# A hop-token graph transformer: a third buffer for the big one-hot of the second bucket pass, shared buffers for its smaller tiles, and slot rows asked for in the other order

## The chip, the cores and the metric

The kernel runs on one core of one Trainium2 chip. The metric is the device time of one execution in microseconds (us); the time given is the median of several runs. A profile comes from one execution more, taken by the hardware profiler.

## What is computed

The reference, cut to what matters (N = 10000 nodes, E = 160000 edges with random ends, D = 128, K = 7):

```python
h = x
toks = [x]
for _ in range(K):
    msg = h[src] * deg_inv_sqrt[src, None] * deg_inv_sqrt[dst, None]
    h = _segment_sum(msg, dst, N)
    toks.append(h)
tok = jnp.stack(toks, axis=1)                      # (N, K+1, D)
t = _layernorm(tok, axis=-1)
# q, key, v = t @ wq, t @ wk, t @ wv
attn = _softmax(jnp.einsum('nkd,nld->nkl', q, key) * scale, axis=-1)
o = tok + jnp.einsum('nkl,nld->nkd', attn, v) @ wo
alpha = _softmax(jnp.einsum('nkd,d->nk', _layernorm(o, axis=-1), w_r), axis=-1)
return jnp.einsum('nk,nkd->nd', alpha, o)
```

Seven times the rows of the nodes are gathered by src, weighted, and summed by dst; then each node's eight tokens go through one attention block and a weighted sum.

## The kernel before

The edges never move as rows. They are sorted once into buckets, and each hop is then done by matmuls with one-hot matrices. Four stretches follow one another:

- **First bucket pass** (`pass_a`): edges are bucketed by the 128-node tile of dst; there are 79 such tiles (NT). `decode` turns the result into keys.
- **Second bucket pass and first hop**, interleaved (`run`, the loop over quads). This is where the change lies.
- **Hops 2 to 7**: for each tile a matrix w is loaded, rows of the table are gathered with it by matmuls (L608), copied from PSUM (eb, L613 and L615) and summed into the tile (acc, L583).
- **Attention**, with an order of its own written out by hand.

In the second pass the edges of each dst tile are bucketed again by blocks of the source node (76 buckets, NS, of 32 slots, CAP). Tiles are taken in *quads* of four, and a quad is placed as two *pairs*. `place` does a quad. For each pair, with DVE unless another engine is named: the big one-hot `oh` (128 x 25 x 76 x 2, in two buffers) by `onehot` (L213) from the keys; PE counts it (ur, L430, L436), ACT copies the counts (H, U2); in `rank` the product `ux` of oh and U2 (L226), PE sums it (L230, L231), DVE reduces it to the ranks rk (L234); the one-hot `rob` of the ranks (L213), and its two products with the slot values, both halves of `R` (L219). Then PE places: `tb` = oh x R in 50 small matmuls (L449), and ACT copies tb (tbs, L450). At the end of the quad the slot rows go to DRAM (`srow`, L459), and a handful of overflow edges per tile is treated with small steps and two one-hots `ohp` (L493).

`matrices` builds for each of the 79 tiles the matrix w that the hops use: it reads the tile's slot row back, spread over all partitions, in two pieces `ra` (two buffers) and `rb` (one buffer), both asked for on SP's queue (L517). rb becomes a part of w on DVE (L524), ra two parts on ACT (L529), dsl another on DVE (L532), and w is written to DRAM (gsd, L534). `hop1` runs the first hop over the finished tiles of an earlier quad (`block`, `fin1`).

Three generators, placing quad q+1, building the matrices of quad q and the first hop of quad q-1, are stepped in turn, 16 rounds a quad:

```python
for i in range(16):
    if i % 3 != 1:
        next(pl, None)
    if i % 4 < 3:
        next(mt, None)
    next(hp, None)
```

One tile of `matrices` is three steps: L524 with the request of the next tile's row and half of L529; the other half; L532 with the write of w. One tile of the hop is four steps.

This order is only a preference. When the kernel is built, a list scheduler lays the instructions of each engine in a fixed order by estimated durations, buffers that come free and, among those ready, place in the program. Each engine then works off its list in order and waits on semaphores.

Pools: `bwp` holds two buffers of each of its tiles, `bw1` one. A tile is known by its name, or by its tag where one is given; tiles of one tag share the buffers.

Of the kernel before, what the change touches and what calls it, by code (L numbers as in the profile page):

```python
# [8 lines left out]
F16 = mybir.dt.float16  # L9
# [19 lines left out]
NCH = NCOL // B  # L29
CAP = 32  # L30
NJ = NG + NI
NS = 4 * NJ
# [4 lines left out]
KO = 8  # L37
# [10 lines left out]
class Hops:  # L48
# [158 lines left out]
            V.tensor_copy(self.q2, q[:, 0:1])  # L207


    def onehot(self, pool, name, key, n):  # L210
        m = key.shape[1]
        oh = pool.tile([128, m, n, 2], F16, name=name)
        self.nc.vector.tensor_tensor(oh, key[:, :, None, :].to_broadcast([128, m, n, 2]),  # L213
                                     self.io2[:, None, :n, :].to_broadcast([128, m, n, 2]), op=ALU.is_equal)
        return oh
# [4 lines left out]

    def rank(self, wp, wu, R, oh, U2, w):

        nc, T = self.nc, self.nc.tensor
        m, nk, k = oh.shape[1], oh.shape[2], 5
        ux = wu.tile([128, m, nk, 2], F16, name="ux")
        nc.vector.tensor_tensor(ux, oh, U2[:, None].to_broadcast([128, m, nk, 2]), op=ALU.mult)  # L226
        R = R[:, :m * k * 2].rearrange("p (j k i) -> p j k i", k=k, i=2)
        for s in range(0, nk, k):
            e = min(k, nk - s)
            T.matmul(R[:, :, :e, :], self.id16, ux[:, :, s:s + e, :], start=s == 0, stop=False, skip_group_check=True)  # L230
        T.matmul(R[:, :, 0, :], self.id16, w, start=False, stop=True, skip_group_check=True)  # L231
        rk = wp.tile([128, m, 2], F16, name="rk")
        with nc.allow_low_precision("whole numbers; those over 2048 only have to stay large"):
            nc.vector.tensor_reduce(rk, R.rearrange("p j k i -> p j i k"), axis=X, op=ALU.add)  # L234
        return rk
# [182 lines left out]
    def place(self, ts, got):  # L418

        tc, nc, V, A, T, G = self.tc, self.nc, self.nc.vector, self.nc.scalar, self.nc.tensor, self.nc.gpsimd  # L420
        wp, w1, n = self.bwp, self.bw1, len(ts)
        tbs = wp.tile([NS, 4, 64], F16, name="tbs")
        ov = wp.tile([128, 4, 8], F32, name="ov")
        for p0 in range(0, n, 2):
            cols = lambda z: z[:, :, ts[0] + p0:ts[0] + p0 + 2]
            oh = self.onehot(wp, "oh", cols(self.kB), NS)
            ur = self.pU.tile([128, 512], F32, name="ur")
            H = wp.tile([128, NS, 2], F16, name="H")
            for c in range(NCH):
                T.matmul(ur[:, :2 * NS], self.id16, oh[:, c], start=c == 0, stop=c == NCH - 1)  # L430
            A.copy(H, ur[:, :2 * NS].rearrange("p (k i) -> p k i", i=2))
            yield
            U = ur[:, 512 - 2 * NS:].rearrange("p (k i) -> p k i", i=2)
            h = NS // 4
            for w in range(4):
                T.matmul(U[:, w * h:(w + 1) * h], self.triw[:, w, :], H[:, w * h:(w + 1) * h], start=True, stop=True)  # L436
            U2 = wp.tile([128, NS, 2], F16, name="U2")
            A.copy(U2, U)
            yield
            rk = self.rank(wp, w1, ur, oh, U2, cols(self.wB))  # L440
            ro = self.onehot(w1, "rob", rk, CAP)
            R = w1.tile([128, NCH, 2 * CAP, 2], F16, name="R")
            self.times(R[:, :, :CAP], ro, cols(self.sl))
            self.times(R[:, :, CAP:], ro, cols(self.dl))
            yield
            tb = self.psm.tile([NS, 2, 64], F32, name="tb")
            for g in range(2):
                for c in range(NCH):
                    T.matmul(tb[:, g, :], oh[:, c, :, g], R[:, c, :, g], start=c == 0, stop=c == NCH - 1)  # L449
            A.copy(tbs[:, p0:p0 + 2, :], tb)  # L450
            vo = wp.tile([128, NCH, 2], F32, name="vo")
            V.scalar_tensor_tensor(vo, rk, float(CAP), cols(self.TT), op0=ALU.is_ge, op1=ALU.mult)
            for g in range(2):
                V.max(ov[:, p0 + g, :], vo[:, :, g])
            yield
        n, a, b = len(ts), ts[0], ts[-1] + 1
        msc = self.psm.tile([128, 128], F32, name="msc")

        nc.sync.dma_start(self.srow[a:b, :].rearrange("t (s r) -> s t r", r=CAP), tbs[:4 * NG, :n, 0:CAP])  # L459
        dsl = wp.tile([128, 4, NJ], F16, name="dsl")  # L460
        for g in range(n):
            for q in range(4):
                T.matmul(msc[32 * q:32 * q + 32, 32 + g * NJ:32 + (g + 1) * NJ], tbs[:, g, CAP:2 * CAP], self.esel[:, q, :],
                         start=True, stop=True, tile_position=(0, 32 * q))
                T.matmul(msc[32 * q:32 * q + 32, 16 + g * NI:16 + (g + 1) * NI], tbs[:, g, 0:CAP], self.esel[:, q, NG:],
                         start=True, stop=True, tile_position=(0, 32 * q))
        A.copy(dsl[:, :n, :], msc[:, 32:32 + n * NJ].rearrange("p (g j) -> p g j", j=NJ))
        V.tensor_scalar(self.oidx[:, a:b, :NI], msc[:, 16:16 + n * NI].rearrange("p (g i) -> p g i", i=NI), -1.0, 0.0, op0=ALU.add, op1=ALU.max)
        got.append(dsl)
        n = 4  # L470

        fl = wp.tile([128, 4, 8], F16, name="fl")
        V.tensor_scalar(fl[:, :n], ov[:, :n], 0.5, None, op0=ALU.is_gt)
        ct = wp.tile([128, 4], F16, name="ct")
        with self.nc.allow_low_precision("counts up to 8"):
            V.tensor_reduce(ct[:, :n], fl[:, :n], axis=X, op=ALU.add)
        T.matmul(msc[:, 0:n], self.tri, ct[:, :n], start=True, stop=True)
        yield
        po = wp.tile([128, 4, 8], F32, name="po")
        V.tensor_tensor(po[:, :n], msc[:, 0:n, None].to_broadcast([128, n, 8]), self.iof1[:, None, :8].to_broadcast([128, n, 8]), op=ALU.add)  # L480
        V.tensor_mul(po[:, :n], po[:, :n], fl[:, :n])
        ph = wp.tile([128, KO, 4], F16, name="ph")
        V.tensor_scalar(ph.rearrange("p k g -> p g k"), po[:, :n, :KO], -1.0, None, op0=ALU.add)
        vi = wp.tile([128, 4, 8, 4], I32, name="vi4")
        V.tensor_scalar(vi[:, :n, :, 3], ov[:, :n], -1.0, None, op0=ALU.add)
        V.tensor_single_scalar(vi[:, :n, :, 0], vi[:, :n, :, 3], 14, op=ALU.arith_shift_right)
        V.tensor_scalar(vi[:, :n, :, 1], vi[:, :n, :, 3], 7, 127, op0=ALU.arith_shift_right, op1=ALU.bitwise_and)  # L487
        V.tensor_single_scalar(vi[:, :n, :, 2], vi[:, :n, :, 3], 127, op=ALU.bitwise_and)
        dg = wp.tile([128, 4, 8, 3], F16, name="dg")
        V.tensor_copy(dg[:, :n, :, 0:2], vi[:, :n, :, 0:2])  # L490
        V.tensor_scalar(dg[:, :n, :, 2], vi[:, :n, :, 2], 1.0, None, op0=ALU.add)
        for g in range(0, n, 2):
            ohp = self.onehot(w1, "ohp", ph[:, :, g:g + 2], 128)  # L493
            for i in range(2):
                for k in range(KO):
                    T.matmul(msc[:, 4 + 3 * (g + i):7 + 3 * (g + i)], ohp[:, k, :, i], dg[:, g + i, k, :], start=k == 0, stop=k == KO - 1)
        yield
        lo = wp.tile([128, 16], F32, name="lo")
        V.tensor_copy(lo[:, :3 * n], msc[:, 4:4 + 3 * n])
        l3 = lo[:, :12].rearrange("p (g k) -> p g k", k=3)  # L500
        n = len(ts)
        V.scalar_tensor_tensor(self.oidx[:, a:b, NI], l3[:, :n, 0], 128.0, l3[:, :n, 1], op0=ALU.mult, op1=ALU.add)
        V.tensor_tensor(self.Sov[:, a:b, :], l3[:, :n, 2:3].to_broadcast([128, n, 128]),
                        self.iof1[:, None, :].to_broadcast([128, n, 128]), op=ALU.is_equal, saturate=False)

    def matrices(self, ts, dsl, W):
# [4 lines left out]
        def row(t):  # L511
            m = 4 * NA * CAP
            ra = self.bwp.tile([128, m], F16, name="ra")
            rb = self.bw1.tile([128, 4 * NG * CAP - m], F16, name="rb")
            r1 = self.srow[t:t + 1, :]
            for r, a in ((ra, 0), (rb, m)):
                nc.sync.dma_start(r, bass.AP(tensor=r1.tensor, offset=r1.offset + a, ap=[[0, 128], [1, r.shape[1]]]))  # L517
            return ra, rb

# [137 lines left out]
    def run(self, ctx, att, nhop=K):  # L657
        tc, nc, V, A, T, G = self.tc, self.nc, self.nc.vector, self.nc.scalar, self.nc.tensor, self.nc.gpsimd
        with ExitStack() as c:
# [46 lines left out]
            for q in range(nq + 1):  # L706
# [5 lines left out]
                for i in range(16):  # L712
                    if i % 3 != 1:
                        next(pl, None)
                    if i % 4 < 3:
                        next(mt, None)
                    next(hp, None)
                for g in (pl, mt, hp):
# [655 lines left out]
```

## Time and profile before

| | |
|---|---|
| median of 3 runs | 3949.62 us (3941.75 to 3951.11) |
| the profiled execution | 3958.33 us, its span 3956.4 us |
| PE busy over the span | 3707.2 us (94%) |
| DVE busy | 3165.6 us (80%) |
| ACT busy | 2812.9 us (71%) |
| POOL busy | 1689.8 us (43%) |
| second pass with first hop, 404 to 1150 us | PE 676.05, DVE 663.59, ACT 551.17, POOL 251.31 us busy |

PE is TensorE, DVE VectorE, ACT ScalarE, POOL GpSimd, SP the engine that issues most DMAs. Busy time is the union of an engine's instructions. A wait is told as "who <- whom": the instruction that stood at the head of its engine, and the one whose end released it, with the idle time in us, the number of times and the longest. A row of the timeline has start and duration in us, engine, line, operation, written <- read tiles, shapes and count; in brackets the idle time ahead of it and what ended it.

### The profile page before, as it was taken

Reading aid. Unit: us, or ns where it says so; the run is one execution under the profiler, and the core shown is the slowest. Engines: PE = TensorE matmul, PEld = TensorE weight load, DVE = VectorE, ACT = ScalarE, POOL = GpSimd, SP = SyncE. Lnnn points to the kernel's source line nnn. Section 1 sums busy time; section 2 is a strip of 40 time slices with the busy share of each in tenths; the row PEclk is TensorE's granted clock in tenths of the full one; section 3 lists DMA queues with packets and bytes.
Section 4 is the critical chain, followed back from the end, with each engine's and each line's share of the span. In section 5 each row is a group of like instructions: output and inputs, shape, how many; then the busy total and the mean of one; then the engine's idle time right before and its main releaser. Section 6 shows DMA issues by size and latency. Waiting matters only on the chain.

```text
span 3956.4 us, 174256 instructions
## 1 busy us (share of the span) xinstructions
PE 3707.2 (94%) x74141; PEld 2992.0 (76%) x74141; DVE 3165.6 (80%) x6888; ACT 2812.9 (71%) x6950; POOL 1689.8 (43%) x2221
## 2 busy tenths in 40 slices
PE   6787899999989999999999999999999998999997
PEld 4665677777768888888888788878878886777775
DVE  8998999998867777777777777777776664888888
ACT  6885577777776666766667677666765657888885
POOL 0000234333345665666566566656656662121111
PEclk8998899999999999999999999999999999999998
DMA  3100454545456666666666666666666653222220
GB/s 101 37 2 1 146 160 152 164 148 158 142 160 191 199 202 194 203 200 203 192 198 203 183 205 203 198 191 198 203 191 202 189 183 98 83 76 84 77 83 18
DMA packets 332729, 595.58 MB, mean 151 GB/s; under 512 B 57447, under 2 KB 215493, under 8 KB 326693
## 3 DMA queue, kind: packets, MB, share of 16 engines
q1 hardware_dynamic: 293989, 506.70, 40.6%
q0 software_dynamic: 35392, 72.55, 6.7%
q8 instruction: 580, 9.50, 1.0%
q10 hardware_dynamic: 2560, 5.12, 0.5%
q14 instruction: 208, 1.70, 0.2%
HBM read 455.49 MB, written 128.67 MB: 148 GB/s over the span
## 4 chain that ended last, share of the span: by engine, by line
PE 72%; DVE 16%; DMA 5%; ACT 3%; issue 2%; SPq 1%; another core or an unknown queue 0%; ACTq 0%; DVEq 0%; POOLq 0%
PE p L608 26%; PE acc L583 23%; PE acc L568 4%; PE pv L1018 4%; PE pu L1002 3%; DMA rb<-srow 2%; DVE o L219 2%; DVE w L532 2%; DVE oh L213 2%; DVE ux L226 2%; PE po L1037 2%; PE tb L449 2%; PE pt L992 2%; PE ps L1067 1%; ACT rs L347 1%
## 5 line engine op out<-in xcount | busy, mean ns | idle before, releaser
L613 ACT ACTIVATE eb<-p 128x512 f16<-128x512 f32 x3065 | 1636.7, 604 | 566.2 <-PE p L608 327.9
L615 DVE TENSOR_TENSOR eb<-p,four 128x512 f16<-128x512 f32 x1912 | 1232.0, 686 | 334.8 <-PE acc L583 201.3
L608 PE MATMUL p<-tab,w 128*32 128x256 f16 x39816 | 1296.2, 275 | 42.8 <-issue 15.3
L608 PEld LDWEIGHTS <-w 128*32 128x32 fp8e4 x39816 | 998.9, 96 | 231.6 <-issue 171.4
L583 PE MATMUL acc<-eb,w 128*128 128x256 f16 x8532 | 1013.6, 273 | 0.7 <-issue 0.7
L583 PEld LDWEIGHTS <-w 128*128 128x128 fp8e4 x8532 | 836.7, 98 | 99.9 <-issue 1.3
L544 POOL DMA_INDIRECT og<-tabh,oidx x553 | 626.1, 1132 | 662.3 <-DVE vi L487 388.3
L544 POOL DMA_INDIRECT og<-tabd,oidx x541 | 553.4, 1023 | 752.2 <-PE acc L566 311.8
L653 POOL TENSOR_SCALAR r<-s,ctok 128x128 f32<-128x128 f32 x474 | 294.9, 622 | 48.7 <-DVE s L599 31.1
L644 ACT ACTIVATE tab<-s,c 128x128 f16<-128x128 f32 x395 | 158.5, 401 | 204.0 <-DVE eb L615 167.7
L645 DVE SCALAR_TENSOR_TENSOR tab<-s,c,tab 128x128 f16<-128x128 f32 x395 | 138.9, 352 | 180.6 <-issue 168.8
L1107 POOL TENSOR_TENSOR p<-e,in 128x1024 f32<-128x1024 f32 (+1 forms) x40 | 76.5, 1913 | 447.0 <-DVE e L1106 447.0
L1059 ACT ACTIVATE junk<-tab 128x128 f32<-128x128 f32 x626 | 248.6, 402 | 8.4 <-SPq L1343 6.8
L347 ACT ACTIVATE rs<-iof,rb 128x128 fp8e4<-128x128 f32 x784 | 231.8, 389 | 0.3
L599 DVE TENSOR_REDUCE s<-acc 128x128 f32<-128x256 f32 x474 | 196.8, 415 | 24.8 <-PE acc L597 11.7
L558 PE MATMUL acc<-eb,w 128*128 128x129 f16 x1422 | 214.5, 225 | 1.8 <-ACT eb L613 1.7
L532 DVE TENSOR_TENSOR w<-dsl,iof 128x2432 fp8e4<-128x2432 f16 x79 | 211.9, 2683 | 0.8 <-PE acc L559 0.8
L559 PE MATMUL acc<-eb,w 128*128 128x128 f16 x1422 | 210.7, 222 | 0.0
L558 PEld LDWEIGHTS <-w 128*128 128x128 fp8e4 x1501 | 140.1, 98 | 65.8 <-issue 62.9
L543 POOL COPY og<-eb 128x1 f16<-128x1 f16 x452 | 84.1, 186 | 240.2 <-ACT eb L613 240.1
L1018 PEld LDWEIGHTS pv<-Wv,xT 128*64 128x64 f32 x2504 | 138.9, 137 | 44.7 <-ACT uT L1003 29.1
L1018 PE MATMUL pv<-Wv,xT 128*64 128x131 f32 x2504 | 163.6, 280 | 8.4 <-issue 4.6
(299 smaller groups left out, 5048.7 us busy)
## 6 DMA issues: line engine op xcount, KB each, us to landing
w<-gsd SPq DMA_DIRECT2D x474, 592.0 KB
gsd<-w SPq DMA_DIRECT2D x79, 592.0 KB
tok<-r SPq DMA_DIRECT2D x546, 64.0 KB
tab<-tok SPq DMA_DIRECT2D x273, 128.0 KB
tabd<-tab SPq DMA_DIRECT2D x396, 64.0 KB
ra<-srow SPq DMA_DIRECT2D x79, 320.0 KB
rb<-srow SPq DMA_DIRECT2D x79, 256.0 KB
og<-tabh,oidx POOLq DMA_INDIRECT x553
```

What stands on the lines that cost most here:

```text
L347: A.activation(ro[:, j - a, i, :], self.iof, AF.Abs_reciprocal_sqrt, scale=2.0 ** 21, bias=rb[:, j - VP, i:i + 1], saturate=False)
L532: V.tensor_tensor(w[:, :NJ * 128].rearrange("p (j d) -> p j d", d=128), dsl[:, g, :, None].to_broadcast([128, NJ, 128]), self.iof1[:, None ...
L544: self.nc.gpsimd.indirect_dma_start(out=o, out_offset=None, in_=src[0] if i == NI else src[1], in_offset=bass.IndirectOffsetOnAxis(ap=self ...
L558: T.matmul(acc[0][:, :128 + ones], W, rows[:, 128:256 + ones], start=start, stop=False, skip_group_check=True)
L559: T.matmul(acc[0][:, :128], W, rows[:, :128], start=False, stop=False, skip_group_check=True)
L583: T.matmul(acc[0][:, :256], w[:, J * 128:(J + 1) * 128], e[:, j, :256], start=False, stop=J == NG - 1 and not late)
L608: T.matmul(p[32 * q:32 * q + 32, j], w[:, NJ * 128 + s * CAP:NJ * 128 + (s + 1) * CAP], tab[:, s, :], start=True, stop=True)
L613: A.activation(e[:, :n, 0:256], pv, AF.Copy, scale=4.0)
L615: V.tensor_tensor(e[:, :n, 0:256], pv, self.four[:, :, None].to_broadcast([128, n, 256]), op=ALU.mult)
L653: self.nc.gpsimd.tensor_scalar(r, s, ct[:, t:t + 1], None, op0=ALU.mult)
L1018: T.matmul(p[64 * h:64 * h + 64, u - us[0], :], S[i]["xT"][:, h * m + q, 64 * c:64 * c + 64], Wv, start=True, stop=True, tile_position=(0, ...
L1059: A.activation(j, S[i]["x"][:, g, :], AF.Square, bias=S[i]["x"][:, g, 0:1], scale=-1.0, accum_out=R[i % 6][:, 0, g:g + 1])
```

## The change

- `oh` of the second pass gets three buffers instead of two.
- `rob` and `ohp` share one buffer (tag "ohp"), of ohp's size; `R` and `ux` share one buffer (tag "ux"), of ux's size. R is the first 64 of 76 columns of such a tile, so its rows stand 304 bytes apart instead of 256. In bytes per partition: oh 7600 more, rob's 3200 and R's 6400 of their own are no longer needed.
- For each row rb is asked for ahead of ra.
- The steps of `matrices` stand in rounds 1, 2, 3 of each four, instead of 0, 1, 2.

The tiles of `onehot` are allocated flat and viewed in the old shape. The number of instructions and their shapes stay.

```diff
@@ -207,9 +207,9 @@
             V.tensor_copy(self.q2, q[:, 0:1])
 
 
-    def onehot(self, pool, name, key, n):
+    def onehot(self, pool, name, key, n, size=None, **kw):
         m = key.shape[1]
-        oh = pool.tile([128, m, n, 2], F16, name=name)
+        oh = pool.tile([128, size or 2 * m * n], F16, name=name, **kw)[:, :2 * m * n].rearrange("p (m n i) -> p m n i", n=n, i=2)
         self.nc.vector.tensor_tensor(oh, key[:, :, None, :].to_broadcast([128, m, n, 2]),
                                      self.io2[:, None, :n, :].to_broadcast([128, m, n, 2]), op=ALU.is_equal)
         return oh
@@ -222,7 +222,7 @@
 
         nc, T = self.nc, self.nc.tensor
         m, nk, k = oh.shape[1], oh.shape[2], 5
-        ux = wu.tile([128, m, nk, 2], F16, name="ux")
+        ux = wu.tile([128, m, nk, 2], F16, name="ux", tag="ux")
         nc.vector.tensor_tensor(ux, oh, U2[:, None].to_broadcast([128, m, nk, 2]), op=ALU.mult)
         R = R[:, :m * k * 2].rearrange("p (j k i) -> p j k i", k=k, i=2)
         for s in range(0, nk, k):
@@ -423,7 +423,7 @@
         ov = wp.tile([128, 4, 8], F32, name="ov")
         for p0 in range(0, n, 2):
             cols = lambda z: z[:, :, ts[0] + p0:ts[0] + p0 + 2]
-            oh = self.onehot(wp, "oh", cols(self.kB), NS)
+            oh = self.onehot(wp, "oh", cols(self.kB), NS, bufs=3)
             ur = self.pU.tile([128, 512], F32, name="ur")
             H = wp.tile([128, NS, 2], F16, name="H")
             for c in range(NCH):
@@ -438,8 +438,8 @@
             A.copy(U2, U)
             yield
             rk = self.rank(wp, w1, ur, oh, U2, cols(self.wB))
-            ro = self.onehot(w1, "rob", rk, CAP)
-            R = w1.tile([128, NCH, 2 * CAP, 2], F16, name="R")
+            ro = self.onehot(w1, "rob", rk, CAP, 2 * KO * 128, tag="ohp")
+            R = w1.tile([128, NCH, NS, 2], F16, name="R", tag="ux")[:, :, :2 * CAP]
             self.times(R[:, :, :CAP], ro, cols(self.sl))
             self.times(R[:, :, CAP:], ro, cols(self.dl))
             yield
@@ -490,7 +490,7 @@
         V.tensor_copy(dg[:, :n, :, 0:2], vi[:, :n, :, 0:2])
         V.tensor_scalar(dg[:, :n, :, 2], vi[:, :n, :, 2], 1.0, None, op0=ALU.add)
         for g in range(0, n, 2):
-            ohp = self.onehot(w1, "ohp", ph[:, :, g:g + 2], 128)
+            ohp = self.onehot(w1, "ohp", ph[:, :, g:g + 2], 128, tag="ohp")
             for i in range(2):
                 for k in range(KO):
                     T.matmul(msc[:, 4 + 3 * (g + i):7 + 3 * (g + i)], ohp[:, k, :, i], dg[:, g + i, k, :], start=k == 0, stop=k == KO - 1)
@@ -513,7 +513,7 @@
             ra = self.bwp.tile([128, m], F16, name="ra")
             rb = self.bw1.tile([128, 4 * NG * CAP - m], F16, name="rb")
             r1 = self.srow[t:t + 1, :]
-            for r, a in ((ra, 0), (rb, m)):
+            for r, a in ((rb, m), (ra, 0)):
                 nc.sync.dma_start(r, bass.AP(tensor=r1.tensor, offset=r1.offset + a, ap=[[0, 128], [1, r.shape[1]]]))
             return ra, rb
 
@@ -712,7 +712,7 @@
                 for i in range(16):
                     if i % 3 != 1:
                         next(pl, None)
-                    if i % 4 < 3:
+                    if i % 4:
                         next(mt, None)
                     next(hp, None)
                 for g in (pl, mt, hp):
```

## The prediction

> **What bounds the kernel now.** I read the page first, then the engines' busy time by stretches (the columns are the stretch, its length, the busy time of PE, weight loads, DVE, ACT and POOL, the granted clock and the DMA share), then the waits, the chain and the timeline of the stretch that the edit touches.
>
> ```profile
> span 3956.4 us, 174256 instructions
> ```
> ```profile
> 404.00:1150.00 746.00, 676.05 (x13392) 530.55 (x13393) 663.59 (x977) 551.17 (x1148) 251.31 (x152) 0.97 0.50 157
> ```
>
> The edit touches the second bucket pass, which shares its stretch (404 to 1150 us) with the first hop. That is 746 us of 3956; later hops keep their instructions, and in the first pass only the way a tile is named differs. PE is busy for 676 us and DVE for 664 of these 746, so neither is full: DVE lacks 82 us, PE 70. What fills the gaps is read from the waits of the same stretch (us in total, times, longest):
>
> ```profile
> DVE w L524 <- DMA rb<-srow: 30.5, 26, 2.8
> DVE oh L213 <- PE tb L449: 25.6, 20, 3.3
> PE tb L449 <- DVE R L219: 23.1, 23, 2.3
> PE p L608 <- ACT eb L613: 13.4, 26, 2.0
> PE msc L496 <- DVE ohp L213: 12.4, 26, 1.9
> PE p L608 <- ACT w L529: 5.9, 2, 5.1
> PE ur L230 <- DVE ux L226: 2.7, 4, 1.5
> ACT w L529 <- DMA ra<-srow: 26.8, 18, 6.0
> SPq L655 <- ACT r L651: 204.8, 62, 8.8
> ```
>
> Two waits hold 56 of DVE's 82 idle us: the slot row rb (30.5) and the big one-hot oh, which waits for the place matmuls tb (25.6). PE in its turn waits 38 us for DVE (23.1 + 12.4 + 2.7). Whether DVE sets the pace is a matter of the chain of waits; these are pieces of it (start, us, what):
>
> ```profile
> 805.69 2.08 PE tb L449 x50
> 807.79 2.14 DVE oh L213
> ...
> 823.16 0.67 DVE w L524
> 823.85 4.24 DMA rb<-srow
> 828.11 0.75 DVE w L524
> ...
> 831.75 2.00 PE tb L449 x50
> ```
>
> Between 807.8 and 823.8 the chain is almost all DVE, and it leaves DVE just at the two waits: through tb into oh, and through the transfer of rb from one L524 to the next. So these waits are on the path, not beside it. The timeline shows how they arise:
>
> ```profile
> 807.79 2.14 DVE L213 TENSOR_TENSOR oh<-kB,io 128x3800 f16<-128x3800 f16 x1 [0.88 <-PE tb L449]
> ...
> 823.08 0.75 DVE L524 TENSOR_SCALAR w<-rb,pid 128x1024 fp8e4<-128x1024 f16 x1
> ...
> 828.11 0.75 DVE L524 TENSOR_SCALAR w<-rb,pid 128x1024 fp8e4<-128x1024 f16 x1 [1.29 <-DMA rb<-srow]
> 828.78 0.98 DVE L213 TENSOR_TENSOR rob<-rk,io 128x1600 f16<-128x1600 f16 x1
> 829.68 0.20 DVE L452 SCALAR_TENSOR_TENSOR vo<-rk,TT 128x50 f32<-128x50 f16 x1
> 829.81 0.99 DVE L219 TENSOR_TENSOR R<-rob,sl 128x1600 f16<-128x1600 f16 x1
> 830.71 0.98 DVE L219 TENSOR_TENSOR R<-rob,dl 128x1600 f16<-128x1600 f16 x1
> ...
> 831.80 2.12 DVE L226 TENSOR_TENSOR ux<-oh,U 128x3800 f16<-128x3800 f16 x1
> 833.83 2.13 DVE L213 TENSOR_TENSOR oh<-kB,io 128x3800 f16<-128x3800 f16 x1
> ...
> 870.21 2.14 DVE L213 TENSOR_TENSOR oh<-kB,io 128x3800 f16<-128x3800 f16 x1 [1.90 <-PE tb L449]
> ...
> 872.34 2.13 DVE L226 TENSOR_TENSOR ux<-oh,U 128x3800 f16<-128x3800 f16 x1
> ```
>
> After the products R of a pair DVE has one of two orders. Either ux of the next pair follows at once, beside tb (831.80), and oh comes behind it without a wait (833.83); or oh comes first and waits for tb, because with two buffers its own is the one that tb still reads (870.21, 1.90 us), and ux follows (872.34). With the second pair of a quad some small steps lie between R and oh, and 0.88 us of the wait is left (807.79).
>
> **The third buffer.** It adds no instruction. oh of 2.14 us depends on nothing but kB and a free buffer, so with a third one it can be laid into the 2.0 us in which tb runs. The ends: all 25.6 us of DVE idle time go, or none, if the order fills the third buffer earlier and the next oh then waits for tb as before. No other engine is asked for more: PE reads the same tiles.
>
> **The shared buffers.** rob shares with ohp, R with ux. rob is read by DVE alone (the two products behind it, 829.81 and 830.71), and ohp is read by 16 short matmuls far from any rob, so I put nothing on that pair. The cover is that distance; without it a rob would wait for matmuls that now themselves wait for ohp, 12.4 us in 26 places, and that is the end of what it could cost. R and ux are another matter. R is written behind its own ux anyway. But ux of the next pair may now start only when tb has read R, and in the first order above it runs just beside tb. I count nine such places, these being the first and the last of them:
>
> ```profile
> 455.22 2.13 DVE L226 TENSOR_TENSOR ux<-oh,U 128x3800 f16<-128x3800 f16 x1
> ...
> 1066.64 2.12 DVE L226 TENSOR_TENSOR ux<-oh,U 128x3800 f16<-128x3800 f16 x1
> ```
>
> Nine times the 2.00 us of tb is 18 us of new wait, with ux at the head of DVE and rob, L524 and L532 queued behind it, if nothing stands ahead of it. If oh of 2.14 us is laid there, the order is R, oh, ux, and tb's 2.00 us are covered: cost nothing. Between 0 and 18 I take half, 9, since one oh per pair is all there is to lay in and I can't see where the schedule spends it. Together: 25.6 − 9 = 16.6 us gained, with ends of 25.6 gained and 18 lost. R's rows move from a stride of 128 elements to one of 152; the products of the first pass write at a like uneven stride (158) at 814 ns for 1264 elements, the ones here take 987 for 1600, the same rate, so I put nothing on it.
>
> ```profile
> L219 DVE TENSOR_TENSOR o<-oh,d x150: 794/814/901, 41.5 to 343.6; 128x1264 f16<-128x1264 f16 x100, 128x1422 f16<-128x1422 f16 x50
> ```
>
> **The slot rows and the shifted step.** Each L524 waits for rb, which has one buffer and is asked for when the L524 before has ended. By place in the quad the 26 waits are: third tile 14 times, 18.8 us; first tile 10 times, 8.4 us; second tile twice, 3.3 us. First and last of the third tile's, then of the first tile's:
>
> ```profile
> 419.89 0.75 DVE L524 TENSOR_SCALAR w<-rb,pid 128x1024 fp8e4<-128x1024 f16 x1 [0.64 <-DMA rb<-srow]
> ...
> 1136.88 0.75 DVE L524 TENSOR_SCALAR w<-rb,pid 128x1024 fp8e4<-128x1024 f16 x1 [1.43 <-DMA rb<-srow]
> ```
> ```profile
> 407.58 0.75 DVE L524 TENSOR_SCALAR w<-rb,pid 128x1024 fp8e4<-128x1024 f16 x1 [0.36 <-DMA rb<-srow]
> ...
> 1088.46 0.75 DVE L524 TENSOR_SCALAR w<-rb,pid 128x1024 fp8e4<-128x1024 f16 x1 [0.42 <-DMA rb<-srow]
> ```
>
> The steps of the matrices now stand at 1, 2, 3 of each four instead of 0, 1, 2: every one comes a sixteenth of a quad later against placing and hop. For the third tile that means that L524 stands behind the placing step with ux, rk, rob and R and no longer ahead of it (step 9 instead of 8). At 828.11 the rob, vo and both products, 0.98 + 0.20 + 0.99 + 0.98 = 3.2 us, would run while rb is on its way; its longest wait in that place is 2.83 us, so all 18.8 us can go. For the first tile a step is about 746/20/16 = 2.3 us against a longest wait of 1.32, and rb is asked for ahead of ra besides:
>
> ```profile
> 809.68 0.33 SPq L517 DMA_DIRECT2D ra<-srow  x1
> 810.06 0.60 SPq L517 DMA_DIRECT2D rb<-srow  x1
> ...
> 823.15 0.32 SPq L517 DMA_DIRECT2D ra<-srow  x1
> 823.85 0.32 SPq L517 DMA_DIRECT2D rb<-srow  x1
> ```
>
> Here rb gains 0.4 us and ra(0) loses as much, 20 times, 8 us at most on ACT, which waits 26.8 us for ra now; the later step gives back 2.3 us each time, so I put 0. Within a quad the swap does little: the ra at 823.15 was free to go before rb, which had to wait for L524. The order is fixed by a scheduler's estimates, and it can pull an L524 forward again wherever it believes DVE idle; against that end (nothing gained) and the other (27.2, the second tile's 3.3 left) I take two thirds, 18 us, nearer to the gain because the order of the program now says so. SP carries the same transfers; those of the matrices (ra, rb, gsd) move one step behind tok and tabd of the hop. SP already stands 204.8 us for tok, and an rb caught behind it comes late; I count this within the third I don't take. The last w of a quad is finished a step later, but its block comes most of a quad after, which is its cover; the price without it is one step, 2.3 us.
>
> A rule speaks against the swap: the Trainium skill ("DMA: Bandwidth & Descriptors", Queues, rings and completion order) has each DMA engine consume descriptors in ring order, so ra would land behind all of rb and not 0.4 us later. By that rule an estimate for ra's delay is up to the 4.24 us of an rb on the chain, less the 2.3 of the step, 20 times: 39 us more on ACT. Of ACT's 26.8 us for ra PE sees 5.9 now, so some 8 us would reach PE and the gain would be 22 instead of 30, within the same range. The trace before has no rb ahead of its ra, so it can't say yet.
>
> **The sum.** 16.6 + 18 = 34.6 us less idle DVE. PE's waits for DVE (38 us) shrink with it; its waits for ACT (13.4 + 5.9) come next, and they may grow. I let 30 of the 34.6 reach the end. The profiled execution took 3958.3 us (span 3956.4 and 1.9 around it), 0.2% over the median of 3949.6; the same 30 us taken from the two give 3928 for a profile and **3919.6 us** for the median.
>
> **Rivals.** *The order hardly changes* (chance 0.12). The scheduler fills the third buffer early, oh still trails tb, and L524 is pulled forward; only the first tile's 8.4 us go: 3949.6 − 8.4 = 3941. For it: oh already stands two pairs ahead of its place in the program, so the order is the scheduler's; against it: L524 and rb, the longest of DVE's waits, stand at places that the program now moves.
>
> *ux takes over the wait of oh* (slower, 0.20). Place: ux behind R. Price: nine waits of 2.0 us become certain, +18, while oh keeps its 25.6 because all three buffers are full when R is done; with 4 us or so of rb saved, +14: 3964. It decides as soon as ux waits for tb over more than the oh and rb waits that went. For it: 831.80 shows ux there with tb just begun. Against it: a free oh is as long as tb.
>
> *PE has no more to give.* If PE's 676 busy us were its floor, they and the 70 − 38 = 32 us of gaps that are not DVE's make 708, so at most 38 of the 56 could be had, and the time would not go under 3912. The row of the stretch has weight loads busy for 530.55 us only. The Trainium skill ("Perfetto Trace Analysis", Identifying the Most-Contended Engine) calls matmul busy time a poor measure, since matmuls are pipelined, and judges by the weight loads, 71% here; by that the full 56 stays open. This moves no chance, only the low end.
>
> **How the numbers follow.** What a measurement of this kernel can tell from no change is about 0.3%, 12 us. Forecast 0.68: all of that is faster by more, from 3894 (all 56 us) to 3937, around 3920. The first rival, 0.12, lies within 0.3%; the second, 0.20, is slower. The range from 3894 to 3955 takes in the forecast and the first rival and leaves out most of the second.
>
> **What would show it.** Right: DVE's wait of oh for tb below 8 us, of L524 for rb below 12, the stretch about 716 us, DVE busy the same 664, R, oh, ux in that order. Wrong: ux waiting for tb by 15 us or more; L524 still 4 to 5 us behind the one before it in the third tile; ACT's wait for ra well over 27; or PE idle as before, now behind ACT.

## The result, and the profile after

The changed kernel takes 3936.67 us (median of 20 runs, 3926.09 to 3946.62), the kernel before 3947.21 (20 runs, 3940.26 to 3954.18). The ratio is 0.9976, 95% interval [0.9968, 0.9984]: a gain of about 10.5 us, where 30 were forecast. The direction was right and the size was not.

First the span, then the busy time by stretch. The stretch is now given from the first big one-hot of the second pass to the end of the first hop (where L743 begins the next), since the fixed window of the prediction reaches past the end of it in a faster kernel. The rows are of before and of after; columns as in the prediction (PE and DVE are the first and the third busy time, the granted clock the third number from the end).

```profile
span 3933.8 us, 174231 instructions
```
```profile
374.74:1147.47 772.73, 693.54 (x13619) 545.91 (x13619) 686.71 (x1006) 553.11 (x1157) 251.85 (x153) 0.96 0.48 150
```
```profile
378.14:1129.98 751.84, 683.68 (x13643) 537.62 (x13643) 685.90 (x1006) 554.12 (x1159) 242.38 (x153) 0.98 0.48 155
```

DVE does the same 686 us of work. The stretch is 20.9 us shorter, but not all of that is the change: PE's matmuls, 24 more by this count, are busy 9.9 us less at a granted clock of 0.98 instead of 0.96. Outside PE's busy time the stretch lost 772.73 − 693.54 = 79.2 against 751.84 − 683.68 = 68.2 us, 11 us less, about what the medians say. The profiled execution of before (3958.33 us) was 11 us over its own later median, that of after (3935.55) 1 us under.

The waits of that stretch (us in total, times, longest), DVE's first, then PE's and ACT's, to be set beside the prediction's rows:

```profile
DVE oh L213 <- PE tb L449: 24.0, 23, 1.7
DVE w L524 <- DMA rb<-srow: 8.1, 13, 1.6
DVE ux L226 <- PE tb L449: 5.2, 4, 2.0
...
PE p L608 <- ACT eb L613: 16.6, 28, 1.5
PE tb L449 <- DVE R L219: 15.0, 18, 3.5
PE ur L230 <- DVE ux L226: 10.7, 17, 3.4
PE msc L496 <- DVE ohp L213: 8.7, 14, 1.9
PE msc L496 <- DVE indeg L677: 4.5, 7, 1.3
...
ACT w L529 <- DMA ra<-srow: 16.4, 14, 7.1
```

The wait of oh is still there, 24.0 us where 25.6 was to go and under 8 was to be left. The wait for rb fell from 30.5 to 8.1, more than forecast. ux waits for tb by 5.2, well under the 15 that I called wrong. PE's waits for R and for ohp fell by 12, but those for ux rose from 6.0 (before, in this same stretch) to 10.7 and one of 4.5 is new. The timeline shows what became of the third buffer:

```profile
378.14 6.23 DVE L213 TENSOR_TENSOR oh<-kB,io 128x3800 f16<-128x3800 f16 x3 [0.36 <-PE W L272]
...
606.16 2.12 DVE L213 TENSOR_TENSOR oh<-kB,io 128x3800 f16<-128x3800 f16 x1
...
611.28 2.12 DVE L213 TENSOR_TENSOR oh<-kB,io 128x3800 f16<-128x3800 f16 x1
...
613.49 2.12 DVE L213 TENSOR_TENSOR oh<-kB,io 128x3800 f16<-128x3800 f16 x1
...
858.96 0.98 DVE L219 TENSOR_TENSOR R<-rob,dl 128x1600 f16<-128x1600 f16 x1
...
860.58 0.75 DVE L524 TENSOR_SCALAR w<-rb,pid 128x1024 fp8e4<-128x1024 f16 x1 [0.45 <-DMA rb<-srow]
862.05 2.14 DVE L213 TENSOR_TENSOR oh<-kB,io 128x3800 f16<-128x3800 f16 x1 [0.72 <-PE tb L449]
864.10 2.17 DVE L226 TENSOR_TENSOR ux<-oh,U 128x3800 f16<-128x3800 f16 x1
```

All three buffers are filled at the very start of the stretch (378.14). By 613.49, after three oh within 10 us that wait for nothing, oh stands three pairs ahead of what has been placed: the scheduler fills the third buffer early. From then on all three are full when R is done, and oh waits for tb as before (862.05, 0.72 us). The rest of this piece is the order that the rows' edit asked for: L524 (860.58) now stands behind R, with most of rb's transfer over. So the rows' edit seems to have done what it was meant to do and the third buffer not; the runs below take them apart.

### The profile page after: what moved, and what is told of

It is laid out like the page before. It is cut to its first block, busy times and chain, and to the rows that moved or that the text cites. A ratio compares the mean times of both kernels' runs of the same rounds, so it can differ in the third digit from the quotient of the medians.

```text
span 3933.8 us, 174231 instructions
## 1 busy us (share of the span) xinstructions
PE 3693.9 (94%) x74141; PEld 2983.6 (76%) x74141; DVE 3172.3 (81%) x6888; ACT 2812.9 (72%) x6950; POOL 1678.8 (43%) x2221
## 4 chain that ended last, share of the span: by engine, by line
PE 75%; DVE 14%; ACT 4%; DMA 4%; issue 2%; SPq 0%; another core or an unknown queue 0%; ACTq 0%; DVEq 0%; POOLq 0%
PE p L608 27%; PE acc L583 23%; PE acc L568 4%; PE pv L1018 4%; PE pu L1002 3%; DVE ux L226 2%; DVE o L219 2%; PE po L1037 2%; PE pt L992 2%; DVE oh L213 2%; PE tb L449 2%; DVE w L532 2%; PE ps L1067 1%; DVE R L219 1%; PE acc L558 1%
## 5 line engine op out<-in xcount | busy, mean ns | idle before, releaser
L608 PE MATMUL p<-tab,w 128*32 128x256 f16 x39816 | 1291.8, 274 | 39.4 <-ACT eb L613 17.4
L608 PEld LDWEIGHTS <-w 128*32 128x32 fp8e4 x39816 | 997.5, 96 | 223.8 <-issue 169.2
L544 POOL DMA_INDIRECT og<-tabh,oidx x553 | 616.9, 1115 | 655.2 <-DVE oidx L468 394.5
L532 DVE TENSOR_TENSOR w<-dsl,iof 128x2432 fp8e4<-128x2432 f16 x79 | 211.9, 2682 | 2.7 <-PE acc L559 2.7
```

What stands on the lines that cost most here:

```text
L532: V.tensor_tensor(w[:, :NJ * 128].rearrange("p (j d) -> p j d", d=128), dsl[:, g, :, None].to_broadcast([128, NJ, 128]), self.iof1[:, None ...
L544: self.nc.gpsimd.indirect_dma_start(out=o, out_offset=None, in_=src[0] if i == NI else src[1], in_offset=bass.IndirectOffsetOnAxis(ap=self ...
L608: T.matmul(p[32 * q:32 * q + 32, j], w[:, NJ * 128 + s * CAP:NJ * 128 + (s + 1) * CAP], tab[:, s, :], start=True, stop=True)
```

## The experiments

Three theories were set against each other. A: the third buffer is filled early and worth nothing; what gain there is comes from the rows. B: the buffer works and another edit takes the gain away. C: DVE's waits are an effect and not the cause; the stretch is paced by PE working off its list, so what DVE gets back it waits again elsewhere.

The kernels ran on several chips. The time of the kernel before differs between them (3953.8 us for four that were run together, both rows' edits, the step alone, third and shared buffers, oh behind R; about 3917 for the others), so only ratios to the kernel before on the same chip are compared. Rows of traces are set beside each other across chips all the same; outside the stretch the spans differ between them by up to 1% (3181 us with oh behind R, 3149 with shared buffers alone), so differences of a few us between two stretches say little. Where rows of a trace are given, they are of the same stretch, first big one-hot to L743.

### Rows: both edits, the step alone, the swap alone

Kernel before, with both lines (e1_rows), the second only (e2_shift), the first only (e7_swap):

```diff
-            for r, a in ((ra, 0), (rb, m)):
+            for r, a in ((rb, m), (ra, 0)):
...
-                    if i % 4 < 3:
+                    if i % 4:
```

> Only the two edits to the slot rows: rb asked for ahead of ra, matrix steps in rounds 1, 2, 3; oh keeps two buffers, nothing is shared. Theory (the gain is the rows' alone; a third buffer is full from the start, so oh goes on trailing tb): ratio to before 0.996 to 0.9985, as with the whole change (0.9976); DVE's wait for rb near 8 us instead of 30, its wait of oh for tb still 20 to 28 us. Rival (the third buffer earns its part): ratio 0.9985 to 1.000, with more wait of oh for tb than in the whole change (24.0).

> Only the matrix steps in rounds 1, 2, 3. If the moved step is what puts rob and R ahead of the third tile's L524, DVE's wait for rb falls to 8 to 14 us and the ratio is 0.997 to 0.999. If it takes the swap as well (DVE's compiled order has L524 ahead of rob in the steady quads here, as before), the wait for rb stays over 18 us and the ratio is 0.999 to 1.002.

> Only rb asked for ahead of ra. The compiled DVE order still has the third tile's L524 ahead of rob. Theory (it takes swap and shift together to move L524 behind rob and R): DVE's wait for rb 15 us or more, ratio 0.9985 to 1.001. Rival (the swap alone carries the rows' gain): rb's wait under 10 us, ratio 0.9965 to 0.9985.

Measured: both 0.9976 [0.9965, 0.9987], step alone 0.9989 [0.9979, 0.9999], swap alone 0.9991 [0.9982, 1.0001]. DVE's waits with both, then with the step alone, then with the swap alone:

```profile
DVE oh L213 <- PE tb L449: 26.3, 24, 2.3
DVE w L524 <- DMA rb<-srow: 12.9, 21, 2.1
```
```profile
DVE w L524 <- DMA rb<-srow: 26.4, 30, 2.0
```
```profile
DVE oh L213 <- PE tb L449: 15.5, 15, 2.6
DVE w L524 <- DMA rb<-srow: 14.3, 23, 2.1
```

The two lines alone give the whole change's gain. The step alone leaves rb at 26.4 and hardly moves L524, against the prediction, which gave it nearly all and the swap nearly nothing. The swap alone halves rb's wait and takes 10 us from oh's wait for tb (6 of them come back as a wait for PE's ur), and still its gain is not clear of zero. Only with both does the list have the third tile's L524 behind rob and R in most quads. And 17.6 us less waiting for rb made 9.5 us of time.

### Buffers: third and shared, shared alone, all but the third

The three hunks on `oh`, `rob`/`ohp` and `R`/`ux` on the kernel before (e3_buffers); the same without the third buffer (e9_share); the whole change without it (e10_no_third). A third buffer without the sharing has no room in the memory.

```diff
-            oh = self.onehot(wp, "oh", cols(self.kB), NS, bufs=3)
+            oh = self.onehot(wp, "oh", cols(self.kB), NS)
```

> Only the third buffer of oh and the sharing that makes room for it; slot rows as before. Theory: no gain, oh waits for tb 15 to 30 us as before, rb 25 us or more, ratio 0.999 to 1.004. Rival (third buffer earns its part): ratio 0.995 to 0.999, oh's wait for tb under 12 us.

> Only the two sharings: rob with ohp, R with ux; oh keeps two buffers, slot rows as before. In DVE's compiled order ux no longer stands right behind R; L524 and L532 come between in many pairs. Theory (the gain of the two buffer edits without the slot rows, ratio 0.9980, comes from that order and not from the third buffer): ratio 0.996 to 0.9985, DVE's waits for tb under 18 us in all. Rival (sharing is the price of the third buffer): ratio 1.000 to 1.005, ux waiting for tb by 10 us or more.

> The whole change without the third buffer of oh. Theory: the ratio stays within 0.002 of the whole change's 0.9976 or is lower, since the third buffer only moves oh ahead. Rival (the third buffer earns its part): ratio over 0.999.

Measured: third and shared 0.998 [0.997, 0.999], shared alone 0.998 [0.9968, 0.9991]; the whole change without the third buffer 0.9987 [0.9975, 0.9999], which overlaps the whole change's interval. DVE's waits with third and shared buffers, then with shared ones alone, and a piece of the latter's timeline:

```profile
DVE w L524 <- DMA rb<-srow: 21.7, 21, 2.0
DVE ux L226 <- PE tb L449: 16.8, 10, 2.1
DVE oh L213 <- PE tb L449: 8.2, 10, 0.9
```
```profile
DVE w L524 <- DMA rb<-srow: 22.0, 23, 2.3
DVE ux L226 <- PE tb L449: 13.3, 8, 2.0
DVE oh L213 <- PE tb L449: 11.3, 13, 1.6
```
```profile
710.71 0.98 DVE L219 TENSOR_TENSOR R<-rob,dl 128x1600 f16<-128x1600 f16 x1
...
711.79 2.67 DVE L532 TENSOR_TENSOR w<-dsl,iof 128x2432 fp8e4<-128x2432 f16 x1
714.38 2.13 DVE L213 TENSOR_TENSOR oh<-kB,io 128x3800 f16<-128x3800 f16 x1
716.43 2.13 DVE L226 TENSOR_TENSOR ux<-oh,U 128x3800 f16<-128x3800 f16 x1
```

Beside the sharing the ratio is the same with the third buffer or without it; the theory for e3_buffers (no gain) missed, because the sharing gains, as e9_share shows, and not because the third buffer does. In the whole change it differs by 0.0011 (0.9987 against 0.9976), some 4 us, which the two intervals do not tell from nothing; without it oh waits 11.8 us for tb and another 10.9 for PE's count ur (L436), with it 24.0 for tb. The sharing, for which I had put down a loss, is itself a gain of 0.2%. oh's wait halves, but ux, which waited for no tb before, takes its place: 13.3 and 11.3 are 24.6 us behind tb, against 25.6. With the third buffer as well the sum is 25.0, and ux has most of it. So the gain does not come out of the waits for tb; rb's wait fell from 30.5 to 22.0, but whether that is the gain is not shown. In places the list now covers tb with another step: L532 of 2.67 us (711.79), behind which oh and ux follow without a wait. That is what the trace shows; that the scheduler does it because ux must now wait for tb is argued.

Rows alone give 0.24%, sharing alone 0.2%, the whole change 0.24%. They do not add. With the rows' edit DVE's list after R is L524, oh, ux (862.05 above), and oh again waits 24 us; that this is why they do not add is not shown.

### oh queued behind R

The whole change, with oh of a pair held back, on DVE's list alone, until the products of the pair two before it are issued. Then its buffer has long been free and it cannot trail tb (its lines are numbered 2 higher from there on: L526 is L524).

```diff
-            oh = self.onehot(wp, "oh", cols(self.kB), NS, bufs=3)
+            with tc.issue_after(self.Rs[-2]) if len(self.Rs) > 1 else ExitStack():
+                oh = self.onehot(wp, "oh", cols(self.kB), NS, bufs=3)
...
-            self.times(R[:, :, CAP:], ro, cols(self.dl))
+            self.Rs.append(self.times(R[:, :, CAP:], ro, cols(self.dl)).ins)
```

> The whole change, and the oh of pair P is queued on DVE behind the last product R of pair P-2, so that the third buffer is not filled ahead of time but used in the time of tb. Theory (the third buffer gives nothing because it is filled early): DVE's wait of oh for tb falls from 24.0 us to under 3, and 12 to 24 us of it reach the end: ratio to before 0.991 to 0.995. Rival (DVE's wait for tb is not on the path, PE or ACT take its place): the wait goes but the ratio stays at 0.996 to 0.999.

Measured: 0.9975 [0.9965, 0.9986], that of the whole change. Its stretch, its waits and a piece of its timeline:

```profile
377.74:1129.90 752.16, 679.07 (x13643) 533.53 (x13643) 687.56 (x1006) 556.95 (x1159) 299.62 (x153) 0.98 0.49 155
```
```profile
DVE rk L234 <- PE ur L231: 15.5, 16, 3.3
DVE w L526 <- DMA rb<-srow: 14.7, 21, 1.2
DVE lo L501 <- PE msc L498: 10.4, 14, 1.7
...
ACT w L531 <- DMA ra<-srow: 37.3, 20, 5.5
```
```profile
909.82 0.98 DVE L219 TENSOR_TENSOR R<-rob,dl 128x1600 f16<-128x1600 f16 x1
...
910.96 2.13 DVE L213 TENSOR_TENSOR oh<-kB,io 128x3800 f16<-128x3800 f16 x1
```

This is the third buffer as the prediction meant it: oh right behind R, no wait (910.96), and no row "oh behind tb" in the stretch at all. The stretch is as long as after's, 752.16 against 751.84 us. The 24 us have come back, as waits for other steps of PE, rk for the rank sums (15.5; after 4.2) and lo for msc (10.4; after 3.0), and as a longer wait for rb (14.7 for 8.1). So a buffer that works gives nothing that this run can resolve (0.0001 by the medians, some 5 us either way by the intervals); what was expected of the run, 12 to 24 us, missed, and its rival came. Of B this leaves little, though not nothing: the sharing is in every kernel with a third buffer, and what such a buffer would give without it can't be run. For C it is a strong run, but PE is not the only engine left: ACT's wait for ra grew from 16.4 to 37.3 us in the same list.

### Less work for DVE, less work for PE

Whole change, the product of rob with the source slots moved from DVE to POOL (e6_dve_less); whole change without that product, tb reading the other product for both halves (e13_no_sl; lines from there on are numbered 1 lower); whole change without the second of the two matmuls by which a matrix's gathered rows are summed in the first hop (e5_pe_less). The last two leave out that part of the computation.

```diff
-            self.times(R[:, :, :CAP], ro, cols(self.sl))
+            G.tensor_tensor(R[:, :, :CAP], ro, cols(self.sl)[:, :, None, :].to_broadcast(list(ro.shape)), op=ALU.mult)
```
```diff
-            self.times(R[:, :, :CAP], ro, cols(self.sl))
...
-     T.matmul(tb[:, g, :], oh[:, c, :, g], R[:, c, :, g], ...
+     T.matmul(tb[:, g, :].rearrange("p (a c) -> p a c", a=2), oh[:, c, :, g], R[:, c, None, CAP:, g].to_broadcast([128, 2, CAP]), ...
```
```diff
-            T.matmul(acc[0][:, :128], W, rows[:, :128], start=False, stop=False, skip_group_check=True)
```

> The whole change, with the product of rob and sl (L219, 40 times 0.99 us) moved from DVE to POOL: 39 us less work for DVE, nothing left out. R is ready later by what POOL takes longer than DVE. Theory (both engines pace it): a gain of 5 to 20 us over the whole change, ratio 0.992 to 0.9965, and DVE waits more for PE. Rival 1 (DVE alone): 30 us or more, ratio under 0.990. Rival 2 (PE alone): no gain, ratio 0.997 to 1.000.

> The whole change, and the product of rob and sl (L219, 40 times 0.99 us) is left out; tb takes the product with dl for both halves, so the slot rows are wrong and with them the hops. DVE has 39 us less to do, PE the same number of matmuls, POOL nothing more. If both engines pace the stretch: 10 to 25 us less than the whole change, ratio to before 0.991 to 0.995. If DVE alone does: 30 us or more, ratio under 0.990. If PE alone does: ratio 0.9965 to 0.999.

> The whole change, and the first hop leaves out the matmul of the high halves (L559), 1500 matmuls at 56 ns, some 83 us less work for PE between 404 and 1130 us; the results of the hops are wrong by that. Theory (PE, in the order of its list, paces the stretch as much as DVE; the freed waits of DVE turn into waits for PE): the stretch gets 25 us or more shorter, ratio to before 0.985 to 0.992, and DVE's waits fall. Rival (DVE alone paces it, with its 24 us of oh behind tb on the path): under 10 us from it, ratio 0.995 to 0.998.

Measured: product on POOL 1.0285 [1.027, 1.0299]; product left out 0.9984 [0.9974, 0.9994]; matmul left out 0.9894 [0.9878, 0.991]. The stretches and DVE's waits, product left out, then matmul left out:

```profile
376.95:1132.77 755.82, 694.49 (x13643) 538.35 (x13643) 651.94 (x966) 549.75 (x1159) 329.55 (x153) 0.98 0.49 154
```
```profile
DVE oh L213 <- PE tb L448: 44.3, 28, 2.9
DVE w L523 <- DMA rb<-srow: 15.1, 24, 1.8
```
```profile
376.79:1106.14 729.35, 644.09 (x12210) 477.94 (x12213) 677.18 (x1006) 545.90 (x1164) 310.63 (x153) 0.94 0.50 159
```
```profile
DVE lo L499 <- PE msc L496: 18.1, 15, 2.5
DVE rk L234 <- PE ur L231: 8.6, 10, 3.5
DVE oidx L468 <- ACT tbs L450: 7.6, 9, 0.9
```

DVE has 34 us less to do without the product (651.94 against 685.90), and the time does not fall below the whole change's; oh just waits longer for tb, 44.3 instead of 24.0. More than the one product changed with the list: PE's busy time is 11 us longer and ACT's wait for ra 45.3 us. Without the second matmul PE runs 1580 matmuls fewer in the whole kernel and is busy 40 us less in the stretch (644.09 against 683.68; 83 had been expected). DVE's work stays nearly the same (677.18). The stretch is 22.5 us shorter, although it counts only 1433 matmuls fewer, and so holds some 150 that in after come behind the stretch. The whole kernel is faster than the whole change by 0.0082 of 3917.7, or 32 us (some 7 either way by the two intervals). The wait "oh behind tb" is gone there without any edit to oh. Neither run holds the order: every kernel here is laid out afresh, and lists of different order differ by 0.3% or so (below). So these two show which engine's work counts, not how much each us of it is worth. The first came out where I had put "PE alone" and not where I had put "both engines".

The run on POOL missed: I wanted DVE lightened and got both slowed. Its groups, POOL's product first, then DVE's beside it (busy, mean ns):

```profile
L443 POOL TENSOR_TENSOR R<-rob,sl 128x1600 f16<-128x1600 f16 x39 | 135.0, 3461 | 66.6 <-DVE vo L452 59.5 <-PE p L608 6.6 <-DVE oidx L502 0.3
```
```profile
L219 DVE TENSOR_TENSOR R<-rob,dl 128x1600 f16<-128x1600 f16 x38 | 49.0, 1289 | 0.0
...
L473 DVE TENSOR_SCALAR fl<-ov 128x32 f16<-128x32 f32 x20 | 39.6, 1980 | 0.2
```

The product takes POOL 3.46 us instead of DVE's 0.99, and tb waits for it (53.5 us in the stretch). It tells nothing of DVE's weight in the time.

### The room for another buffer

Sharing frees 9.6 kB a partition. The prediction's longest wait was that for rb, which has one buffer, so here the room goes to a second buffer for rb:

```diff
-            rb = self.bw1.tile([128, 4 * NG * CAP - m], F16, name="rb")
+            rb = self.bwp.tile([128, 4 * NG * CAP - m], F16, name="rb")
```

On the kernel before with both sharings (e12_share_rb2), with both and the step (e8_rb2), with the rob/ohp sharing only (e11_rb2_alone); and, with `ct` cut to one buffer to make room, with both sharings and the third oh (e14_third_rb2), and on the whole change (e15_all_rb2).

> The room that sharing frees goes to a second buffer for rb and not to a third for oh; matrix steps in rounds 1, 2, 3; ra asked for ahead of rb as before. DVE's compiled order has R, L532, oh, ux in the steady quads, so L532 (2.68 us) covers tb (2.0). Theory (both engines pace it): DVE's waits for rb and for tb fall under 8 us each, the ratio still stays at 0.995 to 0.998. Rival (DVE paces it): ratio under 0.993.

> A second buffer for rb, and rob and ohp sharing one to make room; R and ux apart, two buffers of oh, matrix steps and requests as before. Theory: DVE's wait for rb falls under 5 us, the wait of oh for tb stays over 10 us, ratio 0.994 to 0.998, so the rows are worth about 15 us. Rival (the freed wait for rb comes back as waits for PE): ratio 0.998 to 1.000.

> The best so far without its moved step: both sharings, a second buffer for rb, two of oh, matrix steps in rounds 0, 1, 2 and ra first. If the step adds nothing once rb has two buffers: ratio 0.993 to 0.9955, as with it (0.9941). If it is needed: ratio 0.9965 or more.

> Both sharings, a second buffer for rb and the third for oh (room for it from one buffer less of the small tile ct); steps and requests as before. It stands against the same without the third buffer (0.9941). Theory (the third buffer gives nothing, also with rb's waits gone): ratio 0.993 to 0.9955. Rival (it pays once rb is out of the way): ratio under 0.9925.

> The whole change and a second buffer for rb (ct with one buffer). DVE's wait for rb goes from 8 us to under 4, and its order has L532 behind R in the first pairs. Theory (what counts is that L532 or L524 stands in the time of tb, and that rb doesn't hold up L524): ratio 0.993 to 0.996. Rival (the rows' edits had taken all that rb can give): ratio 0.9965 to 0.998.

| second rb buffer, with | ratio to before |
|---|---|
| rob/ohp shared | 0.9972 [0.9963, 0.9981] |
| both shared | 0.9941 [0.9929, 0.9954], 3894.03 us where before takes 3916.94 |
| both shared, step | 0.9941 [0.9927, 0.9954] |
| both shared, third oh | 0.9944 [0.993, 0.9957] |
| whole change | 0.9978 [0.9969, 0.9987] |

The best one's waits and stretch:

```profile
DVE ux L226 <- PE tb L449: 13.8, 8, 2.5
DVE oh L213 <- PE tb L449: 10.6, 13, 0.9
...
DVE w L524 <- DMA rb<-srow: 4.5, 8, 1.1
```
```profile
378.82:1116.85 738.03, 673.41 (x13611) 532.87 (x13610) 685.04 (x1006) 550.56 (x1155) 305.22 (x152) 0.99 0.49 157
```

Both sharings and a second rb buffer, with neither the third oh nor the rows' edits, beat both kernels: 23 us under the one before, about twice the gain of the change. Here sharing (0.2%) and the rb buffer (0.28%, with one sharing) come to at least their sum. The third oh buffer adds nothing to it (0.9944 against 0.9941), which repeats e3_buffers against e9_share. And with the rows' edits and the third buffer on top the second rb buffer gains nothing over the change (0.9978 against 0.9976), and rb waits 11.6 us there, not under 4 as expected and no less than in the change (8.1); 10.6 of them are the first tile's of a quad. Neither the step alone (0.9941) nor the third buffer alone (0.9944) spoils the gain of the second rb buffer. What is left is the swap or a combination, which was not run, and I cannot derive it from waits. Two more expectations missed here: DVE's waits for tb in e8_rb2 did not fall under 8 us (ux 14.6, oh 10.6), and e15_all_rb2 stayed at the rival's ratio.

## Why the prediction failed in size

**The third buffer: the failed step.** "With a third one it can be laid into the 2.0 us in which tb runs" was put at all 25.6 us. Of oh's wait 24.0 us are left, and the buffer gave nothing that the runs can resolve: third or no third buffer makes no difference beside the sharing (0.998 and 0.998) nor beside the second rb buffer (0.9944 and 0.9941), and in the whole change 0.0011, within the intervals. The other end, "the order fills the third buffer earlier", had been named and was not weighed against the first. That oh "already stands two pairs ahead of its place in the program", as the first rival said, was the sign: this list fills buffers as early as it can, so it keeps one more of them full, and from then on oh waits as before.

**The conversion: the step that failed more.** "I let 30 of the 34.6 reach the end", because "these waits are on the path". The chain of waits does go through them, but it is one chain, and taking a wait out of it does not show how long the next one is. The runs showed that the next is nearly as long. Rows: 17.6 us of rb's wait gone, 9.5 us of time. oh behind R: 24 us of oh's wait gone, no time gained. DVE with 34 us less work: no time gained. PE with 40 us less: some 32. DVE's idle time is the stretch less its 686 us of work, so it gets smaller whenever the stretch does; that it is what sets the stretch was the prediction's assumption, and these runs speak against it.

**The shared buffers: wrong sign.** Nine us of loss, measured a gain of 0.2% alone. The wait of ux itself came, 13.3 us between the 0 and 18 allowed, but it took the place of oh's wait and did not come on top. That the cost can't be under zero was taken for granted: I had no reason to exclude that a constraint improves a list.

**The rows: right in waits, half in time, wrong in parts.** 18 us less waiting for rb were forecast, 22.4 came. The third tile's wait went, as worked out (18.8 before, 2.4 after); the first tile's, which I took to go too, fell only from 8.4 to 5.8. But the step alone leaves 26.4: the swap, of which I had said that it does little, is needed with it. Why it takes both was not tested. ACT's wait for ra did not rise in the change: 26.8 before, 16.4 after; with the swap alone 32.6, and those 5.8 us more are within the 8 at most that I had worked out from the issue times. The 39 us more on ACT estimated by the rule on descriptor order in the Trainium skill ("DMA: Bandwidth & Descriptors", Queues, rings and completion order) were not seen in either. Three times in after both engines waited for the transfers of one tile: DVE's step began at 413.19, 655.17 and 806.32 us, ACT's 0.81, 1.05 and 1.01 us later. So ra does land behind rb, as the order of the requests has it, but by about 1 us and not by the 4.24 of a whole rb; that it would be all of that was my inference. In other kernels with the swap ACT's wait for ra was between 13.9 and 56.1 us, in those without it between 18.0 and 30.4; how much of that spread is the swap was not taken apart.

**The rivals.** "The order hardly changes", at 3941, came nearest. It was right for oh, wrong in its reason for rb, where it was the first tile's wait that stayed and 22.4 us that went; so that its time was near is in part luck. "ux takes over" did not come in the change: 5.2 us in four places, not 18 in nine. With the buffers alone (e3_buffers) it did come, 16.8 us in ten places, but in place of oh's wait (8.2 left), and the kernel was not slower. "PE has no more to give" was the one I underweighted. I let it move no chance because weight loads were busy for 71% only, by the Trainium skill ("Perfetto Trace Analysis", Identifying the Most-Contended Engine). After the change that share is still 72% (537.62 of 751.84), and yet it was PE's work that counted and DVE's that did not. Neither share told which. A likely reason, not tested, is that PE works off its list in order, so a matmul that waits holds back those behind it.

**What stays open.** Why PE as it is does not close its remaining 68 us of gaps. They are spread over waits for DVE (R 15.0, ux 10.7, ohp 8.7, indeg 4.5) and ACT (eb 16.6), no one of which is large. Nor are PE's matmuls a floor at 752 us: the best version does nearly the same ones (13611 of 13643) in 738.03, on another chip. How much of C is PE and how much ACT, whose waits for ra also changed from list to list, was not taken apart. To tell the engines' weights apart, the lists would have to be held fixed while one duration changes, which no run here does.

## What to carry to other kernels

One more buffer can pay where what is written into it comes too late in the list now; where, as here, a list scheduler already issues the step as soon as its buffer is free, the extra one is filled once and the wait stays. Before a wait is counted as time, look at the waits of the engine on its other end: where two engines wait for each other in many small places, a wait taken out of one can come back as another, and here half of it arrived, or nothing. Memory was better spent here on the tile whose transfer is waited for (rb), though not in every combination; each has to be tried, since gains of a relaid list need not add.

## What the hardware did that was not expected

- The product that takes DVE 0.99 us took POOL 2.9 to 3.65 us, and DVE's steps beside it were stretched: the other product from 0.98 to a mean of 1.29 (longest 4.02), a 32-element L473 from 0.18 in after to 1.98 us. DVE's busy time in the stretch rose from 685.90 to 724.47 us though 40 products had left it. Why they were stretched was not tested.
- Without the second matmul the granted clock in the stretch was lower, 0.94 against 0.98 (0.97 with the swap alone, on the same chip), and the gathering matmul L608 (L607 there) took longer. The rows are of after, then of the kernel with fewer matmuls, between 404 and 1090 us:

```profile
L608 PE MATMUL p<-tab,w 128*32 128x256 f16 x4984 | 224.8, 277 | 16.4 <-ACT eb L613 15.1 <-ACT w L529 1.1
```
```profile
L607 PE MATMUL p<-tab,w 128*32 128x256 f16 x5296 | 264.4, 284 | 30.5 <-ACT eb L612 24.0
```

  284 ns for 277. That the lower clock took part of what less work for PE could give is argued from these rows, not shown.
